# One issue order for all loads and copies of a recurrence-and-experts kernel, with the token numbers placed ahead of the gates

## The chip, the core and the metric

The kernel runs on one core of one Trainium2 chip. The metric is device microseconds of one execution, the median of three runs. TensorE is called PE here, VectorE DVE, ScalarE ACT, GpSimd POOL; SyncE (SP) computes nothing and issues DMA transfers.

## What is computed

The reference, cut to what matters:

```python
x, f_logit: (4, 5056, 256)          # batch, seq, d_model; all float32
sig = 1 / (1 + exp(-f_logit));  f = lower_bound + (1 - lower_bound) * sig;  i = 1 - f
for t in range(S):                  # a recurrence along the sequence
    h = f[:, t] * h + i[:, t] * x[:, t];  y[:, t] = h
x = y.reshape(20224, 256)           # tokens of the second half
logits = x @ w_gate                 # w_gate: (256, 8)
expert_idx = argmax(logits);  gate_w = softmax(logits)[expert_idx]
out = zeros((20224, 256))
for e in range(8):                  # w1: (8, 256, 1024), w2: (8, 1024, 256)
    tok_idx = tokens of e, the 80 with the largest gate_w
    out[tok_idx] = gate_w[tok_idx, None] * (relu(x[tok_idx] @ w1[e]) @ w2[e])
```

## The kernel before

The work has three stages. **Recurrence**: 40 units of 512 tokens (ten groups of the sequence times four batches). For each, SP loads 512 KB of `f_logit` (L227) and 512 KB of `x` (L229) into a ring of eight 512 KB slots, ACT, POOL, PE and DVE make the states `h_all` (which stay in SBUF, channels on partitions), and PE makes the logits. **Selection**: values per token and expert are turned by PE (`turn`, L440), DVE takes the eight largest of each part (`tops_of`, L447), and from these candidates the rank among rivals (L648, on DVE for the first `BY_DVE` columns and on ACT for the others), the flag `taken` (L654), the place `put` (L668) and, by 60 small PE products (L672), the table `kept`: row 0 holds the column numbers of the 80 tokens of each expert, row 1 their gate values. `trow` (L676) is row 0 as integers; `uncertain` (L567) makes flags for a rare second path. **Experts**: for each of eight, DVE, ACT and POOL copy the 80 token columns from `h_all` one by one (`gather`, L699; each engine first loads its numbers of `trow` into registers), POOL scales them (L711), PE makes the hidden layer (`hidden`, L716: 32 products per half, with weights taken at a stride of `CH` = 4 elements), ACT and DVE apply the relu, PE makes the result (`result`, L738), DVE copies it out of PSUM, and where 128 rows are complete `finish` turns them and multiplies by the gates (L762) and `scatter` writes them to `out` with an indirect DMA of POOL (L765).

The order of code is the order of each engine's queue. In the expert loop it is, for e = 0 to 7: gather(e+2), hidden(e+1), relu(e+1), result(e), scaled(e+2), then finish and, from e = 5 on, scatter. At e = 1 DVE also runs `rows_of` (L531), 14 small instructions that make `goal` (the rows of `out`) and `gates` from `slots`.

**Transfers.** `out` must be zero elsewhere, so besides the inputs 40 copies of zeros go from `out` to `out` (`copied`, L137; one of them, L157, from SBUF). The 32 halves of the weights (`half`, L495; 512 KB each) go to ring slots 1 to 7 in turn, in the order W1(0), W2(0), W1(1), then W1(e+1), W2(e): half number k takes the slot of half k - 7, so it waits until PE has used that. Seven halves (0 to 6) with three copies, then 12 copies (`SELECTING`) stand in SP's queue after the last unit; then each further half with one copy behind it (`more`, L769) until the copies are used up. Three transfers go through ACT's queue instead: `lb` and `wg` at the start (L94, L98), `flat_dram` (L524: `kept`, brought to SBUF as `flat` by ACT at L783, is written to DRAM), and the two reads of `slots` from it (L528).

The transfers of both queues take eight completion semaphores in rotation, and a transfer waits until the earlier one with its semaphore has landed. What is handed out in rotation isn't told by the code alone:

```python
for k, key in enumerate(halves_of[:NSLOT - 1]):      # L508
    if k % 2:
        copied()
    w_sb[key] = half(*key)
for _ in range(SELECTING):                           # 12
    copied()
```

Of the kernel before, what the change touches and what calls it, by code (L numbers as in the profile page):

```python
# [17 lines left out]
P = 128  # L18
# [8 lines left out]
def kernel(  # L27
# [24 lines left out]
    BY_DVE = 6  # L52
# [41 lines left out]
    nc.scalar.dma_start(out=lb, in_=lower_bound.rearrange("(o p) -> p o", p=P))  # L94
# [3 lines left out]
    nc.scalar.dma_start(out=wg[:, :, :E], in_=w_gate.rearrange("(o p) e -> p o e", p=P))  # L98
# [69 lines left out]
    with tc.tile_pool(name="gsm", bufs=1) as gsm:  # L168
# [9 lines left out]
        def masks():  # L178
            col_i = gsm.tile([P, P], I32, name="col_i", tag="ls")
            nc.gpsimd.iota(col_i, pattern=[[1, P]], base=0, channel_multiplier=0)  # L180
            make_identity(nc, ident)
            col_f = gsm.tile([P, P], F32, name="col_f", tag="col_f")
            low = row_i[:, 0:1]
            for k, (one, two, op, op2) in enumerate((
                    (shift_c, 0, ALU.arith_shift_right, ALU.bitwise_or),
                    (C - 1, 0, ALU.bitwise_and, ALU.bitwise_or),
                    (2, 1, ALU.arith_shift_right, ALU.bitwise_and),
                    (3, 1, ALU.arith_shift_right, ALU.bitwise_and))):
                nc.vector.tensor_scalar(row_i[:, ds(k + 1, 1)], low, one, two, op, op2)
# [13 lines left out]
            nc.vector.scalar_tensor_tensor(out=row_f[:, 2:3], in0=row_f[:, 4:5], scalar=-8.0,  # L203
                                           in1=row_f[:, 2:3], op0=ALU.mult, op1=ALU.add)
            nc.vector.tensor_scalar(nomlb, lb, 1.0, -1.0, ALU.mult, ALU.add)
            nc.vector.tensor_scalar(omlb, lb, -1.0, 1.0, ALU.mult, ALU.add)
# [12 lines left out]

# [123 lines left out]
        def sums(g0, g1):  # L343
            k = run(g0)
            ex = late_exp[:k, ds(LAST - g0, 1)]
            nc.vector.tensor_reduce(sums_t[:k, g0:g1], ex, AX.X, ALU.add)
# [46 lines left out]
        with tc.tile_pool(name="plg", bufs=1, space=PSUM) as plg, \  # L393
             tc.tile_pool(name="plt", bufs=1, space=PSUM) as plt:
            with tc.tile_pool(name="pss", bufs=2, space=PSUM) as pss, \
                 tc.tile_pool(name="psu", bufs=3, space=PSUM) as psu:
                for n in range(-AHEAD, n_unit):
                    unit(load, n + AHEAD)
                    m = n + AHEAD
                    if m == 3:  # L400
                        clear(early)
                    elif 3 < m < TURN and m % 4 == 3:
                        copied()
                    elif m == n_unit - 1:
                        for _ in range(3):
                            copied()
# [15 lines left out]
                    if n == n_unit - 2:  # L422
                        exponentials(LAST - 1, LAST)
                        for g0 in (0, 4):
                            summed(g0, g0 + 4)
                            valued(g0, g0 + 4, nc.gpsimd)
# [10 lines left out]
            with tc.tile_pool(name="pct", bufs=4, space=PSUM) as pct:  # L437
# [14 lines left out]
                a = turn((0, 4))  # L452
# [3 lines left out]
                tops_of(0)  # L456
                tops_of(2)
                some_of(-1)
                sums(LAST - 1, LAST)
                valued(LAST - 1, LAST, nc.vector)  # L460
                by_token(LAST)
                b = turn((4, 6))
                kept_values(a, 0, 4)
                shifted(LAST, n_grp)
                exponentials(LAST, n_grp)
                tops_of(4)
                c = turn((6, LAST - 1), (LAST - 1, LAST))
                kept_values(b, 4, 6)
                equals(LAST, n_grp)
                choice(LAST, n_grp, nc.vector)  # L470
                tops_of(6)
                sums(LAST, n_grp)
                valued(LAST, n_grp, nc.vector)
                d = turn((LAST, n_grp))
                tops_of(LAST - 1)
                tops_of(LAST)
# [17 lines left out]

    def half(which, e, i):  # L495
# [11 lines left out]
    SELECTING = 12  # L507
# [59 lines left out]
    def uncertain():  # L567
# [12 lines left out]
        nc.vector.tensor_scalar(d[:, 3:4], off[:, 2:3], float(capacity), off[:, 1:2],  # L580
                                ALU.min, ALU.not_equal)

    with tc.tile_pool(name="sel", bufs=1) as sel, \
# [17 lines left out]
        busy(psl, 1, "warm")  # L601
# [56 lines left out]
        nc.tensor.matmul(sums_p[:, 1:3], mates, count, start=True, stop=True)  # L658
        for engine, i, n in ((nc.vector, 0, 2), (nc.gpsimd, 2, 3)):
            engine.tensor_tensor(what[:, ds(i, n)], what[:, ds(i, n)],  # L660
                                 taken.unsqueeze(1).unsqueeze(3).broadcast_to([P, n, DEEP, E]),
                                 ALU.mult)
        off = consts.tile([P, 3], F32, name="off")
        nc.vector.tensor_copy(off, sums_p[:, :3])

        put = sel.tile([P, DEEP, K], BF16, name="put")
        at_slot = bass.AP(ahead.tensor, ahead.offset, [ahead.ap[0], (1, DEEP), (1, K)])
        nc.vector.tensor_scalar(put, at_slot, off[:, 0:1], None, ALU.is_equal)  # L668
        for i, terms_of in enumerate(((0, 1), (2, 3, 4))):
            for j in range(DEEP):  # L670
                for t in terms_of:
                    nc.tensor.matmul(kept[:, i], what[:, t, DEEP - 1 - j], put[:, j],  # L672
                                     start=j == 0 and t == terms_of[0],
                                     stop=j == DEEP - 1 and t == terms_of[-1])
        uncertain()
        nc.vector.tensor_copy(trow, kept[:, 0])  # L676
    selc.release()
# [7 lines left out]
    def experts(again):  # L685
        with tc.tile_pool(name="xp", bufs=3) as xp, \
# [29 lines left out]
            def hidden(e):  # L716
# [3 lines left out]
                ps = []  # L720
                for i in range(2):
                    h_ps = psh.tile([P, CH, K], F32, name="h_ps", tag="h_ps")
                    for c in range(CH):
                        for o in range(DC):
# [13 lines left out]
            def result(e):  # L738
                y_ps = psy.tile([P, DC, K], F32, name="y_ps", tag="y_ps")
                halves = [w.pop((2, e, i)) for i in range(2)]  # L740
                hid = HID.pop(e)
                for o in range(DC):
                    for c in range(FC):
                        for s in range(2):
                            nc.tensor.matmul(  # L745
                                y_ps[ds(s * H, H), o],
                                halves[c // CH][:, c % CH, ds(o * P + s * H, H)], hid[:, c],
                                start=c == 0, stop=c == FC - 1, skip_group_check=True)
                at = e * K % YR
                n = min(K, YR - at)  # L750
                nc.vector.tensor_copy(turned_y[:, :, ds(at, n)], y_ps[:, :, :n])  # L751
                if n < K:
                    nc.vector.tensor_copy(turned_y[:, :, ds(0, K - n)], y_ps[:, :, n:])
# [39 lines left out]
            if not again:  # L793
                read_slots()
# [3 lines left out]
            for e in range(E):  # L798
# [10 lines left out]
                if e == 1 and not again:  # L809
                    rows_of(consts)  # L810
# [3 lines left out]
                while e and (done + 1) * P <= (e + 1) * K:  # L814
# [99 lines left out]
```

## Time and profile before

| what | value |
|---|---|
| runs | 253.94, 254.63, 252.56 us; median 253.94 us |
| the profiled execution's own time | 252.7 us |
| its span, first to last instruction | 250.9 us |
| busy share of the span | PE 74%, DVE 64%, POOL 57%, ACT 53% |
| chain that ended last, by engine | PE 32%, DMA 32%, ACT 10%, DVE 9%, issue 8% |
| DMA | 80.66 MB, mean 322 GB/s |

The span is what the trace shows; 1.8 us of the profiled time lie around it. The recurrence lasts to about 127 us, the selection to 145 us, the experts and the scatters to the end. All times below are us from the span's start. SPq, ACTq, DVEq and POOLq are the instruction queues of these engines, in which DMA issues and register loads are seen.

### The profile page before, as it was taken

The numbers are of one execution on the slowest core, as the hardware profiler recorded it, in microseconds if no ns is written. First come the engines' busy times: TensorE is split into PE (matmuls) and PEld (weight loads), VectorE is DVE, ScalarE is ACT, GpSimd is POOL, SyncE is SP. The second block draws the span as 40 slices with busy tenths as digits, with TensorE's granted clock in tenths as the row PEclk, the third lists the DMA queues.
The fourth block names the chain that finished last, engine by engine and source line by source line (L and its number), as shares of the span: only waits on it lengthen the run. The fifth ranks groups of instructions, "written<-read, shape, count | busy, mean of one in ns | idle before, by whom it ended". The sixth has DMA issues, their size and how long they took to land.

```text
span 250.9 us, 7294 instructions
## 1 busy us (share of the span) xinstructions
PE 186.1 (74%) x2452; PEld 155.7 (62%) x2452; DVE 159.4 (64%) x404; ACT 132.9 (53%) x421; POOL 141.8 (57%) x286
## 2 busy tenths in 40 slices
PE   0798899899999998999956787570038859699920
PEld 1686777678768786877734446470037748689810
DVE  5288798999999999989988845414003741525210
ACT  4677787778887887888832445650005235050000
POOL 4778797889788878979662345652200045042121
PEclk9999999999999999999995997777558797899995
DMA  5999999999999999999870005889999999998310
GB/s 179 415 415 434 391 428 393 416 410 408 409 406 410 410 412 415 422 360 464 350 281 0 4 0 180 329 246 303 289 353 433 413 434 406 404 373 270 121 47 27
DMA packets 19686, 80.66 MB, mean 322 GB/s; under 512 B 4392, under 2 KB 4392, under 8 KB 19016
## 3 DMA queue, kind: packets, MB, share of 16 engines
q1 hardware_dynamic: 17520, 79.44, 81.4%
q0 software_dynamic: 240, 0.66, 0.7%
q8 instruction: 21, 0.34, 0.6%
q10 hardware_dynamic: 1880, 0.02, 0.4%
q14 instruction: 25, 0.20, 0.3%
HBM read 78.92 MB, written 21.37 MB: 400 GB/s over the span
## 4 chain that ended last, share of the span: by engine, by line
PE 32%; DMA 32%; ACT 10%; DVE 9%; issue 8%; POOL 3%; ACTq 2%; DVEq 1%; POOLq 0%; SPq 0%
DMA w_sb<-in_moe_w_dram 17%; PE sp L243 11%; PE up L251 9%; PE lg L281 6%; DMA f_t<-in_f_logit_dram 6%; ACT h_all L260 4%; ACT xe L707 3%; DMA out_dram<-out_dram 3%; DMA x_t<-in_x_dram 2%; DMA out_dram<-y,goal 2%; PE lt L305 2%; DVE h_all L268 2%; ACTq L703 2%; PE h_ps L727 2%; ACT ls L290 2%
## 5 line engine op out<-in xcount | busy, mean ns | idle before, releaser
L237 POOL TENSOR_TENSOR x_t<-f_t,x_t 128x1024 f32<-128x1024 f32 x40 | 94.9, 2373 | 21.6 <-DMA x_t<-in_x_dram 13.9
L268 DVE TENSOR_TENSOR_SCAN h_all<-h_all,up 128x512 f32<-128x512 f32 (+1 forms) x80 | 95.8, 1243 | 13.6 <-PE up L251 8.3
L727 PE MATMUL h_ps<-xe,w_sb 128*64 128x80 f32 x512 | 35.8, 319 | 29.5 <-DMA w_sb<-in_moe_w_dram 25.6
L260 ACT ACTIVATE h_all<-sp,nomlb 128x512 f32<-128x512 f32 (+1 forms) x80 | 50.1, 676 | 10.9 <-PE sp L243 10.9
L727 PEld LDWEIGHTS h_ps<-xe,w_sb 128*64 128x64 f32 x512 | 33.5, 222 | 31.9 <-DMA w_sb<-in_moe_w_dram 25.7
L233 ACT ACTIVATE f_t<-f_t 128x1024 f32<-128x1024 f32 x40 | 42.3, 1058 | 14.7 <-DMA f_t<-in_f_logit_dram 11.7
L243 PE MATMUL sp<-ident,f_t 128*128 128x128 f32 x320 | 45.2, 286 | 5.7 <-ACT f_t L233 5.7
L251 PE MATMUL up<-ident,x_t 128*128 128x128 f32 x320 | 44.3, 279 | 5.5 <-POOL x_t L237 3.2
L243 PEld LDWEIGHTS sp<-ident,f_t 128*128 128x128 f32 x320 | 35.8, 145 | 13.6 <-issue 12.5
L251 PEld LDWEIGHTS up<-ident,x_t 128*128 128x128 f32 x320 | 36.3, 142 | 9.0 <-POOL x_t L237 4.8
L707 ACT COPY xe<-h_all 128x2 f32 x256 | 25.4, 191 | 20.7 <-issue 20.2
L707 POOL COPY xe<-h_all 128x2 f32 x192 | 24.4, 193 | 14.7 <-issue 13.3
L707 DVE COPY xe<-h_all 128x2 f32 x192 | 22.7, 172 | 12.7 <-issue 12.7
L711 POOL TENSOR_TENSOR xe<-xe,omlb 128x160 f32<-128x160 f32 x8 | 3.6, 453 | 44.2 <-DVE xe L707 36.1
L281 PE MATMUL lg<-h_all,wg 128*32 128x128 f32 (+1 forms) x640 | 26.3, 282 | 0.0
L735 ACT ACTIVATE hid<-h_ps 128x320 f32<-128x320 f32 x8 | 3.5, 436 | 42.0 <-issue 36.4
L736 DVE TENSOR_SCALAR hid<-h_ps 128x320 f32<-128x320 f32 x8 | 3.9, 491 | 30.1 <-PE h_ps L727 30.1
L745 PE MATMUL y_ps<-hid,w_sb 128*64 128x80 f32 x512 | 21.7, 246 | 0.9 <-DMA w_sb<-in_moe_w_dram 0.8
L745 PEld LDWEIGHTS y_ps<-hid,w_sb 128*64 128x64 f32 x512 | 20.8, 149 | 1.6 <-DMA w_sb<-in_moe_w_dram 1.4
L281 PEld LDWEIGHTS lg<-h_all,wg 128*32 128x32 f32 x640 | 15.5, 108 | 6.1 <-issue 4.9
L751 DVE COPY turned_y<-y_ps 128x160 f32<-128x160 f32 (+1 forms) x8 | 2.6, 320 | 16.9 <-PE y_ps L745 16.9
L765 POOL DMA_INDIRECT out_dram<-y,goal x5 | 5.1, 1021 | 12.4 <-DMA out_dram<-y,goal 6.4
(127 smaller groups left out, 114.8 us busy)
## 6 DMA issues: line engine op xcount, KB each, us to landing
f_t<-in_f_logit_dram SPq DMA_DIRECT2D x40, 512.0 KB, 6.9
x_t<-in_x_dram SPq DMA_DIRECT2D x40, 512.0 KB, 7.2
out_dram<-out_dram SPq DMA_DIRECT2D x38, 512.0 KB, 9.0
w_sb<-in_moe_w_dram SPq DMA_DIRECT2D x32, 512.0 KB, 9.7
out_dram<-h_all SPq DMA_DIRECT2D x1, 512.0 KB
out_dram<-out_dram SPq DMA_DIRECT2D x1, 256.0 KB, 9.1
out_dram<-y,goal POOLq DMA_INDIRECT x5, 2.6
slots<-flat_dram ACTq DMA_DIRECT2D x2, 2.5 KB, 2.6
```

The lines of the kernel that those rows point to most:

```text
L233: nc.scalar.activation(s_t, s_t, ACT.Sigmoid, scale=-1.0)
L237: nc.gpsimd.tensor_tensor(u_t, sts[n], u_t, ALU.mult)
L243: nc.tensor.transpose(ps[:, ds(r * P, P)], sts[n][:, r, ds(o * P, P)], ident)
L251: nc.tensor.transpose(ps[:, r::R], uts[n][:, r, ds(o * P, P)], ident)
L260: nc.scalar.activation(columns(n, o).rearrange("p (k r) -> p k r", r=R), sps.pop((n, o)).rearrange("p (r k) -> p k r", r=R)[:, P - run(n / ...
L268: nc.vector.tensor_tensor_scan(h, h, ups.pop((n, o)), h_all[:, o, ds(spot(n - B) + G - 1, 1)] if n >= B else 0.0, ALU.mult, ALU.add)
L281: nc.tensor.matmul(lgs[g][ds(q * LC, LC), b, :k].rearrange("p (m i) -> p m i", i=2), wg[:, o], pairs[:, :, q], start=o == 0, stop=o == DC ...
L290: nc.scalar.copy(lss[g].rearrange("p (b t) -> p b t", b=B)[:, b0:b1], lgs[g][:, b0:b1, :k])
L707: copy(X[e][:, :, ds(k + j, 1)], h_all[:, :, ds(v, 1)])
L727: nc.tensor.matmul(h_ps[ds(s * H, H), c], wo[o][:, at:at + CH * (H - 1) + 1:CH], xt[:, o], start=o == 0, stop=o == DC - 1, skip_group_chec ...
L745: nc.tensor.matmul(y_ps[ds(s * H, H), o], halves[c // CH][:, c % CH, ds(o * P + s * H, H)], hid[:, c], start=c == 0, stop=c == FC - 1, ski ...
L765: nc.gpsimd.indirect_dma_start(out=out, out_offset=bass.IndirectOffsetOnAxis(ap=goal[:, ds(t, 1)], axis=0), in_=rows[0][:, t % R], in_offs ...
```

## The change

It has these parts.

1. `lb`, `wg`, `flat_dram` and `slots` are issued by SP: the first two after the loads of unit 1 (`small_loads`), `flat_dram` after 14 copies (`SELECTING` is 14 now) and ahead of half 7, and the reads of `slots` at e = 1, between halves 16 and 17.
2. `rows_of` moves from e = 1 to e = 3, and with it the first `finish`: two of them run at e = 3.
3. In the selection `placed(0, ...)` (24 products for the column numbers) goes ahead of `trow`, and `placed(1, ...)` (36 for the gates) behind it; POOL's share of the product with `taken` goes to DVE. One more rank column is ACT's (`BY_DVE` 5), a PE filler product goes ahead of the last `turn`, the sums and values of groups 4 to 7 and the order of the last group's steps change, and all `tops_of` follow each other. `flat` is one ACT copy.
4. For experts 4 to 7 a half of W2 is loaded as two blocks with runs of 2 KB per partition in place of 4 KB, and `hidden` takes W1 at a stride of 2 elements.
5. The last half is loaded as two transfers, the last `result` goes chunk by chunk over both output parts, and ACT copies one of the two.

```diff
-    BY_DVE = 6
+    BY_DVE = 5
-    nc.scalar.dma_start(out=lb, in_=lower_bound.rearrange("(o p) -> p o", p=P))
-    nc.scalar.dma_start(out=wg[:, :, :E], in_=w_gate.rearrange("(o p) e -> p o e", p=P))
+        def small_loads():
+            nc.sync.dma_start(out=lb, in_=lower_bound.rearrange("(o p) -> p o", p=P))
+            nc.sync.dma_start(out=wg[:, :, :E], in_=w_gate.rearrange("(o p) e -> p o e", p=P))
+            nc.vector.tensor_scalar(nomlb, lb, 1.0, -1.0, ALU.mult, ALU.add)
+            nc.vector.tensor_scalar(omlb, lb, -1.0, 1.0, ALU.mult, ALU.add)
...
                     m = n + AHEAD
+                    if m == 1:
+                        small_loads()
...
+    def rows_of_w2(e):
+
+        return CH if e < E // 2 else CH // 2
+
     def half(which, e, i):
...
-            nc.sync.dma_start(out=t, in_=w2[e][ds(i * FH, FH)].rearrange(
-                "(p j) d -> p (j d)", j=CH))
-            t = t.rearrange("p (j d) -> p j d", j=CH)
+            j = rows_of_w2(e)
+            to = t.rearrange("p (a x) -> p a x", x=j * D)
+            of = w2[e][ds(i * FH, FH)].rearrange("(a p j) d -> p a (j d)", p=P, j=j)
+            parts_of = CH // j if (e, i) == (E - 1, 1) else 1
+            for a in range(0, CH // j, CH // j // parts_of):
+                part = ds(a, CH // j // parts_of)
+                nc.sync.dma_start(out=to[:, part], in_=of[:, part])
+            t = t.rearrange("p (c d) -> p c d", d=D)
...
-    SELECTING = 12
+    SELECTING = 14
...
-        nc.scalar.dma_start(out=flat_dram.rearrange("(i e) k -> e i k", e=E), in_=flat)
+        nc.sync.dma_start(out=flat_dram.rearrange("(i e) k -> e i k", e=E), in_=flat)
...
-            nc.scalar.dma_start(out=slots[:, i], in_=flat_dram[ds(i * E, E)].rearrange(
+            nc.sync.dma_start(out=slots[:, i], in_=flat_dram[ds(i * E, E)].rearrange(
...
+        def with_taken(i, n):
+            nc.vector.tensor_tensor(what[:, ds(i, n)], what[:, ds(i, n)],
+                                    taken.unsqueeze(1).unsqueeze(3).broadcast_to([P, n, DEEP, E]),
+                                    ALU.mult)
...
+        placed(0, 0, 1)
+        with_taken(2, 3)
         uncertain()
         nc.vector.tensor_copy(trow, kept[:, 0])
+        placed(1, 2, 3, 4)
...
+                J = rows_of_w2(e)
...
-                                at = i * FH + c + CH * s * H
+                                at = i * FH + a * J * P + j + J * s * H
                                 nc.tensor.matmul(
-                                    h_ps[ds(s * H, H), c], wo[o][:, at:at + CH * (H - 1) + 1:CH],
+                                    h_ps[ds(s * H, H), c], wo[o][:, at:at + J * (H - 1) + 1:J],
...
-                for i in (0, 1):
-                    nc.scalar.copy(flat[:, i], kept[:, i])
+                nc.scalar.copy(flat, kept)
...
                 if e == 1 and not again:
-                    rows_of(consts)
+                    read_slots()
...
-                while e and (done + 1) * P <= (e + 1) * K:
+                if e == 3 and not again:
+                    rows_of(consts)
+                while e >= 3 and (done + 1) * P <= (e + 1) * K:
                     finish(done)
                     done += 1
```

SP's queue after the last unit, in the kernel before, from half 3 (L501) to half 6; L143 are the copies, L499 and L501 the halves of W1 and W2, and in brackets stand the semaphores that an issue waits for:

```order
L501 DMA w_sb<-in_moe_w_dram 128x1024 [waits DMAHW4_49,PE_49,Pool_49]
L499 DMA w_sb<-in_moe_w_dram 128x1024 [waits DMAHW6_49,PE_49]
L143 DMA out_dram<-out_dram 16x8192 [waits DMAHW0_49]
L499 DMA w_sb<-in_moe_w_dram 128x1024 [waits DMAHW1_49,PE_49,Pool_49]
L499 DMA w_sb<-in_moe_w_dram 128x1024 [waits DMAHW2_49,PE_49]
L143 DMA out_dram<-out_dram 16x8192 [waits DMAHW3_49]
```

In this rotation the issue of half 4 holds semaphore DMAHW6, which ACT's queue has for `flat_dram`, and numbers 5 and 7 are left out between rows, since they are ACT's too. The same place after the change, from half 4 (now L505) on, with the copies now L141:

```order
L505 DMA w_sb<-in_moe_w_dram 128x1024 [waits DMAHW4_49,PE_49]
L141 DMA out_dram<-out_dram 16x8192 [waits DMAHW5_49]
L505 DMA w_sb<-in_moe_w_dram 128x1024 [waits DMAHW6_49,PE_49,Pool_49]
L505 DMA w_sb<-in_moe_w_dram 128x1024 [waits DMAHW7_49,PE_49]
L141 DMA out_dram<-out_dram 16x8192 [waits DMAHW0_49]
```

The semaphores follow each other without a gap, each held by the SP transfer eight places ahead. Behind 14 copies follow, at the end of the selection:

```order
L141 DMA out_dram<-out_dram 16x8192 [waits DMAHW5_49]
L535 DMA flat_dram<-flat 8x2x80 [waits DMAHW6_49,Activation_49]
L505 DMA w_sb<-in_moe_w_dram 128x1024 [waits DMAHW7_49,PE_49]
L141 DMA out_dram<-out_dram 16x8192 [waits DMAHW0_49]
L513 DMA w_sb<-in_moe_w_dram 128x1024 [waits DMAHW1_49,PE_49]
```

The write of `flat_dram`, which waits for ACT's copy `flat`, has moved into SP's queue ahead of half 7 (L505), and all later transfers stand behind it.

DVE at the end of e = 3 (relu, result copied out, gates, then the register loads and the copies of gather(6)) in the kernel before:

```order
L736 TENSOR_SCALAR hid<-h_ps 128x320
L751 COPY turned_y<-y_ps 128x2x80
L762 TENSOR_SCALAR y<-t_ps,gates 128x256
L703 TENSOR_LOAD trow
L707 ISA
```

and after the change, from the last of the steps of `rows_of` on (ten more of them stand between the copy of the result and these):

```order
L568 TENSOR_REDUCE two_f<-past 128x5
L569 TENSOR_TENSOR goal<-far,two_f 128x5
L570 TENSOR_SCALAR gates<-slots 128x5
L571 RECIPROCAL gates<-gates 128x5
L793 TENSOR_SCALAR y<-t_ps,gates 128x256 x2
L721 TENSOR_LOAD trow
```

The 14 instructions of `rows_of` and a second product with the gates have come between the result of expert 3 and DVE's share of gather(6).

## Rows read from the trace of the kernel before

**Rows 1.** The page: GB/s that DMA moved in 40 equal slices of the span.
```profile
GB/s 179 415 415 434 391 428 393 416 410 408 409 406 410 410 412 415 422 360 464 350 281 0 4 0 180 329 246 303 289 353 433 413 434 406 404 373 270 121 47 27
```

**Rows 2.** Waits of SP's queue from 150 us: us in total, times, longest.
```profile
SPq L499 <- DMA flat_dram<-flat: 29.3, 1, 29.3
...
SPq L143 <- DMA slots<-flat_dram: 8.8, 2, 8.7
```

**Rows 3.** Timeline of SP's queue, 118 to 212 us: start, us, queue, line, operation, count.
```profile
122.88 0.33 SPq L501 DMA_DIRECT2D w_sb<-in_moe_w_dram  x1
152.59 0.33 SPq L499 DMA_DIRECT2D w_sb<-in_moe_w_dram  x1
...
172.19 0.33 SPq L499 DMA_DIRECT2D w_sb<-in_moe_w_dram  x1
...
183.82 0.52 SPq L143 DMA_DIRECT2D out_dram<-out_dram  x1
185.69 0.34 SPq L499 DMA_DIRECT2D w_sb<-in_moe_w_dram  x1
...
206.01 0.34 SPq L499 DMA_DIRECT2D w_sb<-in_moe_w_dram  x1
```

**Rows 4.** Stretches: us; PE, PEld, DVE, ACT, POOL busy; PE clock, DMA share, GB/s.
```profile
131.00:134.00 3.00, 0.45 (x1) 0.18 (x1) 2.45 (x10) 1.18 (x4) 0.00 (x0) 0.67 0.01 3
...
172.00:185.00 13.00, 0.00 (x0) 0.00 (x0) 0.59 (x6) 0.00 (x0) 3.46 (x25) 0.54 0.99 309
185.00:208.00 23.00, 17.03 (x290) 15.95 (x292) 9.75 (x69) 7.22 (x66) 3.46 (x25) 0.80 1.00 415
```

**Rows 5.** Waits of PE from 150 us: us in total, times, longest.
```profile
PE h_ps L727 <- DMA w_sb<-in_moe_w_dram: 25.6, 6, 17.9
```

**Rows 6.** Timeline, 136 to 165 us: end of the selection, first expert.
```profile
142.86 2.31 PE L672 MATMUL kept<-put,what 128*8 128x80 bf16 x60 [0.94 <-DVE put L668]
...
145.21 0.23 DVE L676 CAST trow<-kept 8x80 int32<-8x80 f32 x1 [1.40 <-PE kept L672]
...
150.93 0.33 ACT L783 COPY flat<-kept 8x80 f32<-8x80 f32 x2
...
151.66 4.43 PE L727 MATMUL h_ps<-xe,w_sb 128*64 128x80 f32 x64 [2.00 <-POOL xe L711]
...
160.29 4.28 PE L727 MATMUL h_ps<-xe,w_sb 128*64 128x80 f32 x60 [1.68 <-DMA w_sb<-in_moe_w_dram]
```

**Rows 7.** Timeline, 165 to 200 us: result(0), and first and last of 14 `rows_of` instructions.
```profile
164.76 2.85 PE L745 MATMUL y_ps<-hid,w_sb 128*64 128x80 f32 x58
...
192.92 0.16 DVE L540 CAST rcol_i<-slots 128x5 int32<-128x5 f32 x1
...
195.09 0.19 DVE L560 RECIPROCAL gates<-gates 128x5 f32<-128x5 f32 x1
```

**Rows 8.** Timeline, 200 to 251 us: last experts and the five scatters.
```profile
222.91 0.29 DVE L751 COPY turned_y<-y_ps 128x128 f32<-128x128 f32 x1 [1.90 <-PE y_ps L745]
...
223.62 4.07 PE L727 MATMUL h_ps<-xe,w_sb 128*64 128x80 f32 x64
223.74 0.48 DVE L762 TENSOR_SCALAR y<-t_ps,gates 128x256 f32<-128x256 f32 x1 [0.43 <-PE t_ps L760]
225.52 2.80 DVE L707 COPY xe<-h_all 128x2 f32 x24 [1.30 <-issue]
...
227.52 2.38 PE L745 MATMUL y_ps<-hid,w_sb 128*64 128x80 f32 x64
...
229.72 1.21 POOL L765 DMA_INDIRECT out_dram<-y,goal  x1 [0.77 <-issue]
...
235.59 0.97 POOL L765 DMA_INDIRECT out_dram<-y,goal  x1 [4.66 <-DMA out_dram<-y,goal]
...
238.27 0.97 POOL L765 DMA_INDIRECT out_dram<-y,goal  x1 [1.71 <-DMA out_dram<-y,goal]
...
245.49 0.97 POOL L765 DMA_INDIRECT out_dram<-y,goal  x1 [3.08 <-DVEq L827]
```

More of the change, by code (lines that the diff above doesn't have):

```diff
@@ L344, in sums @@
             k = run(g0)
-            ex = late_exp[:k, ds(LAST - g0, 1)]
+            ex = late_exp[:k, ds(LAST - g0, 1)] if g0 >= LAST - 1 else shifts[:k, g0:g1]
             nc.vector.tensor_reduce(sums_t[:k, g0:g1], ex, AX.X, ALU.add)
@@ L423 @@
                         exponentials(LAST - 1, LAST)
-                        for g0 in (0, 4):
-                            summed(g0, g0 + 4)
-                            valued(g0, g0 + 4, nc.gpsimd)
+                        summed(0, 4)
+                        valued(0, 4, nc.gpsimd)
                     unit(logits, n - 1)
@@ L450, in tops_of @@
                     peaks(cts[g0][0], cts[g0][1], i)
-                a = turn((0, 4))
                 aside(LAST, 0, B - 1)
@@ L455 @@
                 aside(LAST, B - 1, B)
-                tops_of(0)
-                tops_of(2)
                 some_of(-1)
+                sums(4, LAST - 1)
                 sums(LAST - 1, LAST)
-                valued(LAST - 1, LAST, nc.vector)
+                valued(4, LAST - 1, nc.gpsimd)
+                valued(LAST - 1, LAST, nc.gpsimd)
                 by_token(LAST)
+                a = turn((0, 4))
+                shifted(LAST, n_grp)
+                exponentials(LAST, n_grp)
                 b = turn((4, 6))
                 kept_values(a, 0, 4)
[L464 to L468, printed above, removed]
                 equals(LAST, n_grp)
                 choice(LAST, n_grp, nc.vector)
-                tops_of(6)
                 sums(LAST, n_grp)
                 valued(LAST, n_grp, nc.vector)
+                c = turn((6, LAST - 1), (LAST - 1, LAST))
+                busy(plt, 1, "lt")
+                kept_values(b, 4, 6)
                 d = turn((LAST, n_grp))
-                tops_of(LAST - 1)
-                tops_of(LAST)
+                for lo, _ in parts:
+                    tops_of(lo)
                 kept_values(c, 6, LAST)
@@ L579, in uncertain @@
                                        op0=ALU.is_le, op1=ALU.mult)
-        nc.vector.tensor_scalar(d[:, 3:4], off[:, 2:3], float(capacity), off[:, 1:2],
+        totals = sel.tile([P, 2], F32, name="totals")
+        nc.vector.tensor_copy(totals, sums_p[:, 1:3])
+        nc.vector.tensor_scalar(d[:, 3:4], totals[:, 1:2], float(capacity), totals[:, 0:1],
                                 ALU.min, ALU.not_equal)
@@ L600 @@
             ("rivals", M), ("rivals2", M), ("sums_p", 4)))
-        busy(psl, 1, "warm")
         for r in (rivals2, rivals):
@@ L657, with placed @@
         nc.tensor.matmul(sums_p[:, 0:1], before, count[:, 0:1], start=True, stop=True)
[L658 to L669, printed above, removed]
+        def with_taken(i, n):
+            nc.vector.tensor_tensor(what[:, ds(i, n)], what[:, ds(i, n)],
+                                    taken.unsqueeze(1).unsqueeze(3).broadcast_to([P, n, DEEP, E]),
+                                    ALU.mult)
+        def placed(i, *terms_of):
             for j in range(DEEP):
@@ L674 @@
                                      stop=j == DEEP - 1 and t == terms_of[-1])
+        with_taken(0, 2)
+        off = consts.tile([P, 1], F32, name="off")
+        nc.vector.tensor_copy(off, sums_p[:, :1])
+        nc.tensor.matmul(sums_p[:, 1:3], mates, count, start=True, stop=True)
+        put = sel.tile([P, DEEP, K], BF16, name="put")
+        at_slot = bass.AP(ahead.tensor, ahead.offset, [ahead.ap[0], (1, DEEP), (1, K)])
+        nc.vector.tensor_scalar(put, at_slot, off, None, ALU.is_equal)
+        placed(0, 0, 1)
+        with_taken(2, 3)
         uncertain()
         nc.vector.tensor_copy(trow, kept[:, 0])
+        placed(1, 2, 3, 4)
     selc.release()
@@ L738, in result, with product @@
             def result(e):
-                y_ps = psy.tile([P, DC, K], F32, name="y_ps", tag="y_ps")
                 halves = [w.pop((2, e, i)) for i in range(2)]
                 hid = HID.pop(e)
[L742 to L748, printed above, removed]
+                last = e == E - 1
+                y = psy.tile([P, DC, K], F32, name="y_ps", tag="y_ps")
+                ys = [y[:, o] for o in range(DC)]
+                if last:
+                    ys[1] = psh.tile([P, CH, K], F32, name="h_ps", tag="h_ps")[:, 0]
+                def product(o, c):
+                    for s in range(2):
+                        nc.tensor.matmul(
+                            ys[o][ds(s * H, H)], halves[c // CH][:, c % CH, ds(o * P + s * H, H)],
+                            hid[:, c], start=c == 0, stop=c == FC - 1, skip_group_check=True)
+                for k in range(DC * FC):
+                    product(*(divmod(k, FC) if not last else reversed(divmod(k, DC))))
                 at = e * K % YR
                 n = min(K, YR - at)
-                nc.vector.tensor_copy(turned_y[:, :, ds(at, n)], y_ps[:, :, :n])
+                if last:
+                    assert n == K
+                    nc.vector.tensor_copy(turned_y[:, 0, ds(at, n)], ys[0])
+                    nc.scalar.copy(turned_y[:, 1, ds(at, n)], ys[1])
+                    return
+                nc.vector.tensor_copy(turned_y[:, :, ds(at, n)], y[:, :, :n])
                 if n < K:
-                    nc.vector.tensor_copy(turned_y[:, :, ds(0, K - n)], y_ps[:, :, n:])
+                    nc.vector.tensor_copy(turned_y[:, :, ds(0, K - n)], y[:, :, n:])
             def finish(t):
@@ L793, in experts @@
             if not again:
-                read_slots()
                 total = psm.tile([1, 4], F32, name="total", tag="total")
```

3 lines of the change are left out of this document (1 added, 2 removed).

## The prediction, made before the change was timed

> **What bounds the kernel now.** I read the page's slices first. DMA moves some 410 GB/s through the recurrence, then nothing for three slices of 6.3 us, then 180 to 350 for six, and full rate again only from slice 31 [rows 1]. The queue's own waits say why: SP waited 29.3 us at one issue of a weight half, and the releaser is the landing of `flat_dram` [rows 2]. In the timeline half 3 goes out at 122.88 and half 4 at 152.59 [rows 3], while DMA is idle by 131 [rows 4]. Half 4 and the copies behind it have nothing to do with `flat_dram`; they share a completion semaphore with it, as the order of the queues shows. The reads of `slots` do the same to two later copies for 8.8 us [rows 2]. So about 22 us of transfers that could have run beside the selection run behind it. The bill comes in the experts: PE waits 25.6 us for weights, 17.9 in one piece [rows 5]. PE's busy share hides this. The path after the selection is thus the DMA stream, and at the end a chain on DVE and POOL.
>
> **Part 1, one order: the stream worked out.** I sum it in span time. Two pitches are needed. A semaphore comes free when the transfer eight places ahead has landed, so spacings of issues are spacings of landings. From 172.19 to 183.82 copies land alone: eight issues, seven gaps, 1.66 us each. From 185.69 to 206.01 halves and copies alternate: 17 issues, 16 gaps, 1.27 each [rows 3]. The rates of the two stretches, 309 and 415 GB/s, agree [rows 4].
>
> At 131 the old stream had ended with half 3. Now half 4, a copy, halves 5 and 6 follow (4 x 1.27 = 5.1) and 14 copies alone (23.2): 159.3. `flat_dram` needs ACT's `flat`, ready at 151.3 before [rows 6], and is tiny, so it is covered by the copies in front of it. Half 7 needs the slot that hidden(0) frees, at 156.1 before [rows 6], also covered. Half 7, copy, half 8, copy: 164.4. Half 9 needs result(0), which ended at 167.6 [rows 7]; of that 1.7 was hidden(1) waiting for weights [rows 6], and the selection gives about 1.7 (below): 164.2, just in time. From there 17 transfers bring half 17, the second of W2(3): 164.4 + 17 x 1.27 = 186.0, and 1.3 for the reads of `slots` between and the landing (bounds 0 and 3): 187.3. Half 31 is 14.5 later in the count: 205.7. All slots on the way are free in time, since each half needs only what PE used seven halves earlier.
>
> A rule speaks against this gain. The Trainium skill ("DMA: Bandwidth & Descriptors", section "Issuing engines are not separate DMA queues") says that transfers run on the same 16 DMA engines whichever engine issues them, and that spreading issues only saves issue time. By that the move is worth next to nothing; it is rival C below. This trace shows the other part: it is not the engines that were shared badly but the waits.
>
> **Part 3, the selection.** 60 products take 2.31 us ahead of `trow` [rows 6]; 24 take 0.9, so 1.4 goes. One rank column fewer on DVE and a filler product fewer ahead of the rivals give some tenths, the product with `taken` for three terms costs DVE some tenths ahead of `trow`. I take 1.7 (bounds 0 and 3). The stream covers most of it: with 0, result(0) frees half 9 at 165.9 and the end is 1.5 later. `lb` landing behind four loads, the order of the last sums, one `flat` copy: half a microsecond either way, covered by the same stream, which is full through the recurrence.
>
> **Part 2, the late `rows_of`.** This costs, and on the path. result(3) waits for half 17, of which only its last three quarters are left then (1.8 of the 2.38 us that 64 result products take [rows 8]): 189.1. DVE copies it out (189.5), runs the 14 instructions, 192.92 to 195.28 in the trace [rows 7], 2.4: 191.9. The first product with the gates (0.48 [rows 8]) ends at 192.4; the second turn needs the one PSUM buffer, so PE turns until 192.9, and hidden(5), whose weights landed some 3 us earlier, stands behind it on PE. Behind the second product (193.4) DVE makes gather(6): 1.30 + 2.80 [rows 8], 197.5. Before, this sat at e = 1 and in gaps.
>
> **Part 4, runs of 2 KB.** Two effects. PE: 64 hidden products take 4.07 us at a stride of 4, 64 result products 2.38 with contiguous weights [rows 8]. The trace has no stride of 2, so hidden(4) to hidden(7) lie between 2.4 and 4.1; I take the middle, 3.2. The Trainium skill ("SBUF — State Buffer", section "Door 1: The DMA port swizzle") gives lines of 16 bytes and full rate from two hits per line. A stride of 2 floats has two, a stride of 4 one; by it hidden falls to 2.4, and the forecast would be 0.8 lower. The trace agrees in so far as stride 4 is the slower. DMA: a transfer with runs of 32 KB was not faster than one with 4 KB [rows 3], so I take 0 for 2 KB. Were each of the eight halves to cost double, half 31 would land at 216, and part 5 plus the scatters would still cover most of it: at most 1.6 later.
>
> **The tail.** hidden(5) 192.9 to 196.1, result(4) to 198.5. From the copy of result(4) to the first scatter the trace has 222.91 to 229.72, 6.8: DVE's copy and gates, its gather(7), POOL's scaling [rows 8]. So scatter 0 goes at 205.4. From there to the end it was 250.9 - 229.72 = 21.2, one scatter behind the landing of the other: 226.6. But scatter 0 to 1 took 5.9 and 1 to 2 took 2.7 [rows 8], and four weight halves were under way at the first. Now the last one lands as scatter 0 starts, so up to 3.2 may go; I take half: 225.0. The profiled time is 1.8 more than its span: **226.8 us**, against 252.7 profiled; the median of the runs is 253.94, within their spread.
>
> Part 5 is worth nothing here: hidden(7) starts after scaling at 204.6, result(7) ends at about 212.6 and its rows are ready by 214.2, while scatter 4 can't go before 205.4 + 15.8 - 1.6 = 219.6. If the scatter chain were shorter by 5 us, it would count.
>
> **Rivals.**
>
> A (forecast, 0.68): 226.8, own range 222 to 231.
>
> B (0.14), the stream is slower. If copies keep 1.66 also between weights, 17 transfers cost 6.6 more: 233.4. For: copies alone, DMA fully busy, ran so [rows 4]. Against: the alternating stretch is the very pattern that comes.
>
> F (0.12), the tail is shorter. If gates and gather(6) find gaps (3.3), hidden takes 2.4 (0.8) and no weight disturbs the scatters (1.6): 221.1. For: in-order queues leave gaps where PE waits. Against: the one PSUM buffer.
>
> C (0.03), the change doesn't do what it says: the issue waits elsewhere, and only the 1.7 of the selection is left: 251.0. For: 23 halves still wait for slots. Against: in the new order no semaphore is shared with a later transfer of another queue.
>
> D (0.03), slower: all 25 later halves now stand behind one issue that waits for ACT's `flat`. From 159.3 on each microsecond that it is late costs one. To lose more than the 26 gained, `flat` would have to come after 185; it came at 151.3 [rows 6], so ACT's gather would have to be held by the busy DMA for 34 us. Transfers ran beside all engines throughout the recurrence [rows 1] without such a hold. If it happened, say at 189, the time is 256.5.
>
> **How the numbers follow.** A, B and F hold 0.94. The range takes in F's 221.1 and B's 233.4: 220.5 to 234. C is within 1% (the runs spread by 0.8%, so about 1% is what a measurement of this kernel can tell from no change), D slower: faster 0.94, same 0.03, slower 0.03.
>
> **What would show it.** DMA at 300 to 415 GB/s without an empty slice from 125 to 200; no wait of SP on `flat_dram` over 10 us, and the write behind 14 copies at about 150; half 7 issued near 155 and not at 172; PE's longest wait for weights under 6 us; `rows_of` near 190 and hidden(5) behind two turns; hidden(4) to (7) at 2.4 to 4.1; scatter 0 near 205 and the next 3 to 6 later. Wrong it would be if slices near 140 to 150 were still empty, if PE waited over 10 us for half 17, or if scatter 4 followed result(7) at once.

## The result and the profile after

The kernel after takes **228.59 us** (median of four runs, 228.2 to 230.06); the kernel before, run beside it, 253.45. The ratio is 0.903, 95% interval 0.897 to 0.909: some 25 us faster. 226.8 was forecast, range 220.5 to 234. The profiled execution took 230.06 us with a span of 228.3. One execution of experiment 8 (234.15 us) and one of experiment 12 (232.79 us) ran slow, and the medians there leave it out.

The page's slices, GB/s of DMA, to hold against [rows 1]:

```profile
GB/s 232 335 422 414 414 409 420 408 412 411 392 416 404 411 376 414 417 409 384 411 455 358 425 434 375 353 333 296 332 400 451 401 334 394 127 366 279 41 44 26
```

The three empty slices are gone. One low slice is new, 127 GB/s, the 35th, from 194 to 200 us. The waits of SP's queue, and of PE, from 120 us on (us in total, times, longest), answer to [rows 2] and [rows 5]:

```profile
SPq L513 <- PE h_ps L747: 10.0, 2, 7.2
...
SPq L505 <- PE h_ps L747: 4.0, 2, 3.6
...
SPq L535 <- ACT flat L813: 0.7, 1, 0.7
```

```profile
PE h_ps L747 <- DMA w_sb<-in_moe_w_dram: 5.4, 4, 2.0
PE y_ps L769 <- DMA w_sb<-in_moe_w_dram: 3.5, 3, 2.0
PE t_ps L791 <- DVE y L793: 2.9, 1, 2.9
```

The 29.3 us for `flat_dram` are gone: its write itself waits 0.7 us for ACT. PE's 17.9 us for weights have become waits of at most 2.0. SP's longest wait ahead of a transfer, 7.2 us, is now for a ring slot that hidden(5) holds, and this is the low slice. The timeline of SP's queue (start, us) answers to [rows 3]:

```profile
123.35 0.33 SPq L505 DMA_DIRECT2D w_sb<-in_moe_w_dram  x1
...
128.75 18.59 SPq L141 DMA_DIRECT2D out_dram<-out_dram  x14
149.07 0.34 SPq L535 DMA_DIRECT2D flat_dram<-flat  x1
153.37 0.36 SPq L505 DMA_DIRECT2D w_sb<-in_moe_w_dram  x1
```

Half 4 goes out at 123.35, not 152.59, and half 7 at 153.37, not 172.19. The timeline of PE around `rows_of`, then of POOL's scatters, answers to [rows 7, 8]:

```profile
186.87 3.46 PE L769 MATMUL y_ps<-hid,w_sb 128*64 128x80 f32 x48 [1.96 <-DMA w_sb<-in_moe_w_dram]
...
193.62 0.62 PE L791 MATMUL t_ps<-ident,turned_y 128*128 128x128 f32 x2 [2.91 <-DVE y L793]
194.17 3.85 PE L747 MATMUL h_ps<-xe,w_sb 128*64 128x80 f32 x64
...
201.00 2.44 PE L747 MATMUL h_ps<-xe,w_sb 128*64 128x80 f32 x64
```

```profile
207.09 1.22 POOL L796 DMA_INDIRECT out_dram<-y,goal  x1 [0.78 <-SPq L858]
211.48 0.98 POOL L796 DMA_INDIRECT out_dram<-y,goal  x1 [3.17 <-DMA out_dram<-y,goal]
215.20 0.97 POOL L796 DMA_INDIRECT out_dram<-y,goal  x1 [2.75 <-DMA out_dram<-y,goal]
219.59 0.97 POOL L796 DMA_INDIRECT out_dram<-y,goal  x1 [3.42 <-DMA out_dram<-y,goal]
223.17 0.97 POOL L796 DMA_INDIRECT out_dram<-y,goal  x1 [2.60 <-DMA out_dram<-y,goal]
```

PE waits 2.9 us for the late gates ahead of hidden(5), which takes 3.85 us; hidden(6), with the same stride, takes 2.44. All four later scatters wait for the landing of the one before: this chain ends the kernel.

### The profile page after: what moved, and what is told of

Read it like the earlier page. It is cut to its first block, busy times and chain, and to the rows that moved or that the text cites. A ratio compares the mean times of both kernels' runs of the same rounds, so it can differ in the third digit from the quotient of the medians.

```text
span 228.3 us, 7296 instructions
## 1 busy us (share of the span) xinstructions
PE 179.4 (79%) x2452; PEld 149.5 (66%) x2452; DVE 160.3 (70%) x404; ACT 133.5 (58%) x423; POOL 140.3 (61%) x283
## 5 line engine op out<-in xcount | busy, mean ns | idle before, releaser
L245 PE MATMUL sp<-ident,f_t 128*128 128x128 f32 x320 | 46.0, 289 | 7.0 <-ACT f_t L235 5.6
L253 PE MATMUL up<-ident,x_t 128*128 128x128 f32 x320 | 45.1, 283 | 4.0 <-DVE h_all L270 2.9
L245 PEld LDWEIGHTS sp<-ident,f_t 128*128 128x128 f32 x320 | 36.4, 147 | 15.1 <-issue 12.7
L253 PEld LDWEIGHTS up<-ident,x_t 128*128 128x128 f32 x320 | 37.2, 145 | 6.9 <-DVE h_all L270 4.4
L747 PE MATMUL h_ps<-xe,w_sb 128*64 128x80 f32 x512 | 28.1, 273 | 7.4 <-DMA w_sb<-in_moe_w_dram 5.4
L747 PEld LDWEIGHTS h_ps<-xe,w_sb 128*64 128x64 f32 x512 | 26.6, 186 | 9.6 <-DMA w_sb<-in_moe_w_dram 4.3
L725 DVE COPY xe<-h_all 128x2 f32 x192 | 22.6, 173 | 12.9 <-issue 10.7
L769 PEld LDWEIGHTS y_ps<-hid,w_sb 128*64 128x64 f32 x480 | 19.9, 149 | 4.2 <-DMA w_sb<-in_moe_w_dram 3.4
L307 PE MATMUL lt<-ident,ls 128*128 128x128 f32 (+1 forms) x40 | 7.5, 310 | 4.3 <-ACT ls L292 4.3
```

Source lines behind the costliest of these rows:

```text
L245: nc.tensor.transpose(ps[:, ds(r * P, P)], sts[n][:, r, ds(o * P, P)], ident)
L253: nc.tensor.transpose(ps[:, r::R], uts[n][:, r, ds(o * P, P)], ident)
L307: nc.tensor.transpose(lts[g0][:k, g - g0, j], ls[:, j::R], ident)
L725: copy(X[e][:, :, ds(k + j, 1)], h_all[:, :, ds(v, 1)])
L747: nc.tensor.matmul(h_ps[ds(s * H, H), c], wo[o][:, at:at + J * (H - 1) + 1:J], xt[:, o], start=o == 0, stop=o == DC - 1, skip_group_check= ...
L769: nc.tensor.matmul(ys[o][ds(s * H, H)], halves[c // CH][:, c % CH, ds(o * P + s * H, H)], hid[:, c], start=c == 0, stop=c == FC - 1, skip_ ...
```

## The experiments

Times are medians; "the kernel after" is 228.59 us.

**1. Before, with `flat_dram` and `slots` on POOL's queue.** Is it the shared completion semaphore, or the one order?

```diff
-        nc.scalar.dma_start(out=flat_dram.rearrange("(i e) k -> e i k", e=E), in_=flat)
+        nc.gpsimd.dma_start(out=flat_dram.rearrange("(i e) k -> e i k", e=E), in_=flat)
...
-            nc.scalar.dma_start(out=slots[:, i], in_=flat_dram[ds(i * E, E)].rearrange(
+            nc.gpsimd.dma_start(out=slots[:, i], in_=flat_dram[ds(i * E, E)].rearrange(
```

> The kernel before, with the write of flat_dram and the reads of slots issued by POOL instead of ACT; POOL has no other transfer that is issued before the scatters. Theory (the half's 29.3 us wait came from completion counts that ACT's transfers share with SP's halves, not from the order of issue): with POOL's transfers counted apart the half no longer waits for flat_dram, half 4 is issued near 124 us where it was 152.6, no slice of the page between 130 and 152 us falls below 250 GB/s, and the time is 228 to 235 us. Rival (what counts is that everything goes through one queue in one order): the gap stays and the time is 248 us or more.

231.2 us, ratio 0.910 (0.907 to 0.913). SP's queue:

```profile
122.33 0.33 SPq L499 DMA_DIRECT2D w_sb<-in_moe_w_dram  x1
...
127.08 15.66 SPq L143 DMA_DIRECT2D out_dram<-out_dram  x12
155.52 0.33 SPq L499 DMA_DIRECT2D w_sb<-in_moe_w_dram  x1
```

Half 4 goes out at 122.33. SP has no wait for `flat_dram` any more. Another issuing engine for three small transfers gives 22.6 of some 25 us, with nothing put in one order, so the shared semaphores were the cause. One detail was missed: the slice from 149 to 155 us falls to 118 GB/s, since 12 copies run out before hidden(0) frees a slot; the change has 14.

**2. After, with the two back on ACT's queue.**

```diff
-        nc.sync.dma_start(out=flat_dram.rearrange("(i e) k -> e i k", e=E), in_=flat)
+        nc.scalar.dma_start(out=flat_dram.rearrange("(i e) k -> e i k", e=E), in_=flat)
...
-            nc.sync.dma_start(out=slots[:, i], in_=flat_dram[ds(i * E, E)].rearrange(
+            nc.scalar.dma_start(out=slots[:, i], in_=flat_dram[ds(i * E, E)].rearrange(
```

> The kernel after, with the write of flat_dram and the reads of slots issued by ACT again; all other parts of the change stay. Theory (this one part makes the gain): SP waits 20 us or more for flat_dram again, the DMA engines have slices near empty before 150 us, and the time is 243 to 252 us. Rival (the numbers ahead of the gates, the shorter runs and the chunks of the last result make a good part of the gain): 235 us or less.

252.12 us, ratio 0.994 (0.991 to 0.997), at the upper edge of what was expected. SP's waits:

```profile
SPq L141 <- DMA flat_dram<-flat: 25.9, 1, 25.9
```

The wait is back, at a copy instead of a half, and all other parts together are worth under 2 us while it stands.

**3. After, with the old end of the selection** (60 products ahead of `trow`, POOL's share, `BY_DVE` 6).

```diff
-    BY_DVE = 5
+    BY_DVE = 6
...
-        with_taken(0, 2)
...
-        placed(0, 0, 1)
-        with_taken(2, 3)
...
-        placed(1, 2, 3, 4)
...
+        for engine, i, n in ((nc.vector, 0, 2), (nc.gpsimd, 2, 3)):
...
+        for i, terms_of in enumerate(((0, 1), (2, 3, 4))):
```

> The kernel after, with the end of the selection as before: all 60 products of the kept rows ahead of the gates' sums, the factor applied in two pieces on DVE and POOL, 6 of the 24 numbers' comparisons as before. Theory (the weights' stream covers the selection): hidden(0) starts about 2 us later, hidden(5) at most 0.7 us later, and the time is 0 to 1 us above the kernel after. Rival (the selection is on the path that sets the end): the whole 2.2 us are lost, 230.5 to 231 us.

230.53 us, ratio 0.909 (0.903 to 0.915). hidden(0) starts 1.4 us later (150.90), hidden(5) 0.8 (195.01). By medians this is 1.9 us, by ratios 0.9 to 1.5, and the intervals overlap: between the two expectations, so the stream covers it in part at most.

**4. After, with 4 KB runs for all experts.**

```diff
-        return CH if e < E // 2 else CH // 2
+        return CH
```

> The kernel after, with runs of 4 KB for all eight experts (the weights of a product lie 4 elements apart, not 2; the last expert's second half is one transfer). Theory (the distance of the weights' elements sets the rate at which PE loads them, while runs of 2 KB cost the transfers nothing): hidden(6) and hidden(7) take 4.0 to 4.2 us where they took 2.44, hidden(5) stays at 3.9 to 4.4, and the time is 2 to 3.5 us above the kernel after, as far as the chain of the scatters doesn't hide it. Rival 1 (the chain of the scatters hides all of it): within 0.7 us. Rival 2 (runs of 2 KB slow the stream by more than they give back): 1 us or more faster.

228.55 us, ratio 0.900 (0.897 to 0.902): no difference. The theory fell to its first rival. PE's timeline from hidden(5), and two of the scatters:

```profile
193.70 4.36 PE L747 MATMUL h_ps<-xe,w_sb 128*64 128x80 f32 x64
...
201.48 4.07 PE L747 MATMUL h_ps<-xe,w_sb 128*64 128x80 f32 x64
```

```profile
207.57 1.21 POOL L796 DMA_INDIRECT out_dram<-y,goal  x1 [0.78 <-issue]
...
222.86 0.97 POOL L796 DMA_INDIRECT out_dram<-y,goal  x1 [2.75 <-DMA out_dram<-y,goal]
```

hidden(6) is 1.6 us longer, yet the last scatter goes as early as in the kernel after: only hidden(5) lies ahead of the first scatter, what follows stands beside the chain. What hidden(5) costs stays open: the execution compared here ran it at TensorE's low clock (3.85 us); against the repeat (experiment 9), where it took 2.44, the last scatter is 1.9 us later, while the medians are equal.

**5 to 8. The tail.** These edits are to the expert loop. In experiment 5 `slots` is read, `rows_of` run and the first rows finished one expert earlier:

```diff
+                if e == 0 and not again:
                     read_slots()
...
-                if e == 3 and not again:
+                if e == 2 and not again:
                     rows_of(consts)
-                while e >= 3 and (done + 1) * P <= (e + 1) * K:
+                while e >= 2 and (done + 1) * P <= (e + 1) * K:
```

> The kernel after, with the read of slots, the products of rows_of and the first turn of finished rows one expert earlier (ahead of hidden(4) instead of hidden(5)). Theory (the late rows_of holds hidden(5) by 3 us, and PE's idle time there is followed by its lower clock): hidden(5) starts by 191.5 us where it was 194.2 and takes 2.4 to 2.6 us where it took 3.85, the slice near 127 GB/s is gone, and the time is 3 to 4.5 us below the kernel after. Rival (the read of slots lands late, so hidden(4) is held instead of hidden(5)): the time is within 1 us.

225.37 us, ratio 0.891 (0.886 to 0.895): 3.2 us less, as expected. The slice with 127 GB/s is gone, and hidden(5) follows the turn at once:

```profile
190.26 0.45 PE L791 MATMUL t_ps<-ident,turned_y 128*128 128x128 f32 x2 [0.43 <-DVE turned_y L782]
190.63 2.44 PE L747 MATMUL h_ps<-xe,w_sb 128*64 128x80 f32 x64
```

In experiment 6 the first scatter goes one expert earlier:

```diff
-                while e + 3 >= E and put_out < done:
+                while put_out < (done if e + 3 >= E else 1 if e + 4 == E else 0):
```

> The kernel after, with the first scatter issued one expert earlier, behind result(4), before result(5). Theory (the five scatters run one after another, each held by the one before, so the end is the first scatter plus 21.2 us): the first scatter starts near 201 to 203 us where it was 207.1, and the time is 3 to 4.5 us below the kernel after. Rival 1 (the end is set by the last result's rows, not by the chain): the last scatter starts at the same time, within 0.7 us. Rival 2 (the scatter disturbs the last weights): 0.5 to 2 us slower.

226.07 us, ratio 0.893 (0.889 to 0.897): 2.5 us less, under the 3 to 4.5 expected, though the first scatter goes 7.4 us earlier (5.7 against the repeat):

```profile
199.67 1.21 POOL L796 DMA_INDIRECT out_dram<-y,goal  x1 [0.78 <-issue]
...
206.55 1.01 POOL L796 DMA_INDIRECT out_dram<-y,goal  x1 [0.74 <-DMA out_dram<-y,goal]
210.83 0.98 POOL L796 DMA_INDIRECT out_dram<-y,goal  x1 [3.28 <-DMA out_dram<-y,goal]
```

The chain sets the end, but its length isn't fixed: 6.9 us from the first scatter to the second, where it was 4.4. The last weights are under way then.

Experiment 7 has both edits.

> Both of the two edits above in one kernel: rows_of one expert earlier and the first scatter one expert earlier. Theory (each takes a hold of its own away from one chain): the gains add up to 6 to 8 us, 220.5 to 222.5 us, unless the last weights set the end: they landed at 210.4, and hidden(7), result(7), the last turn and one scatter with its landing behind them take 2.4 + 2.4 + 1.5 + 5, which bounds the end at about 222. Rival (the two remove the same hold): no better than the better one of the two.

223.71 us, ratio 0.882 (0.877 to 0.887): better than either, 4.9 us in all where 6 to 8 were expected. Again the first two gaps of the chain are long (scatters at 197.81, 203.29, 208.02).

Experiment 8 leaves these out and puts products without use into the loop over `result`'s products `k`:

```diff
                 for k in range(DC * FC):
+                    if e == 3 and k == CH and not again:
+                        busy(psm, 5, "total")
```

> The kernel after, with 5 products without use on PE in the middle of result(3), while it waits for its last weights, so that PE has less idle time there. Theory (PE's idle time ahead of the second half of result(3) is followed by the lower clock, at which its products take 72 ns instead of 37): the granted clock between 186.5 and 190.5 us is 0.9 or more where it was 0.64, rows_of, hidden(5) and the first scatter come 1 to 2 us earlier, and the time is 1 to 2 us below the kernel after. Rival (the lower clock has another cause, or 5 products are too few): the clock there stays near 0.64 and the time within 0.5 us.

229.70 us, ratio 0.907 (0.902 to 0.911): no gain. The clock in result(3) did rise, 48 products took 1.88 us and not 3.46, but the five products took 4.56 us and result(3) ended 1.4 us later than without them. hidden(5) behind its idle wait took 3.62 all the same.

**9 to 12. The chain spread out.** Experiment 9 is the kernel after again, on the chip of the next three; it is called the repeat.

> The kernel after, unchanged, to have it beside the next three on the same chip. Theory and rival alike: 228 to 230 us, ratio to the kernel before 0.90 to 0.906.

228.59 us again, ratio 0.905 (0.900 to 0.910).

In experiment 10 every scatter goes as soon as its rows are finished, on top of experiment 7:

```diff
-                while put_out < (done if e + 3 >= E else 1 if e + 4 == E else 0):
+                while put_out < min(done, e - 2):
```

> The kernel with rows_of and the first scatter one expert earlier, and besides every scatter as soon as its rows are finished: the first behind result(3), then one behind each result. Theory (the end is a chain of five scatters, 4 to 5.5 us each, until the last result's rows become later than the chain): the first scatter starts near 192.5 to 194 us, the first four are done before the last rows are ready, the last one starts near 212.5 to 213.5 us, and the end is 5.5 us behind it: span 218 to 219.5, time 219.5 to 221.5 us. Rival (a scatter on POOL's queue holds the gathers behind it, so hidden(6) and hidden(7) come later): 222.5 us or more.

**219.81 us**, ratio 0.868 (0.864 to 0.873): the fastest kernel here, some 33 us below the one before. What POOL waits for from 185 us on, in the kernel after and here:

```profile
POOL out_dram L796 <- DMA out_dram<-y,goal: 11.9, 4, 3.4
```

```profile
POOL out_dram L796 <- DVE y L793: 9.3, 2, 6.9
...
POOL out_dram L796 <- DMA out_dram<-y,goal: 1.0, 1, 1.0
```

The two waits put down to rows are those of the last two scatters, 3 and 4 (counted from 0). For scatter 3 this is right: its rows are ready at 210.54, it goes at 210.82, and scatter 2 had landed at 209.23. For scatter 4 it is doubtful. The end of the chain that ended last (start, us, what):

```profile
202.88 6.35 DMA out_dram<-y,goal
...
210.82 2.58 DMA out_dram<-y,goal
...
213.96 0.30 POOLq L857
214.25 0.90 POOL out_dram L796
```

Scatter 3 lands at 213.40 and scatter 4 goes 0.77 us later; in the kernel after, too, 0.77 us lie between the landing of scatter 3 (222.40) and the start of scatter 4 (223.17), and there its rows had long been ready. So the chain is broken once, ahead of scatter 3, and its last link still stands. The first scatter goes at 188.47, 4 us earlier than expected, and the first three land after 6.2 to 6.5 us, where 4 to 5.5 were expected. The gathers weren't held: hidden(6) and hidden(7) start as in experiment 5. The last scatter goes at 214.17, 0.7 later than expected, behind a stop of PE of 1.85 us in result(6) for which the profile shows no releaser (see the last section).

Experiment 11 adds the edit of experiment 4 to it.

> The kernel with rows_of and all scatters early, and runs of 4 KB for all eight experts. Theory (the distance of the weights' elements sets the length of hidden, and its gain was hidden only by the chain of scatters): hidden(5) to hidden(7) take 4.0 us each where they take 2.44, all of it ahead of the last scatter, so 4 to 5 us slower than with runs of 2 KB, 224 to 226 us. Rival (the stream of weights or the gathers give back what PE loses): within 1.5 us of it.

222.54 us, ratio 0.879 (0.875 to 0.884): with the chain broken ahead of scatter 3 the stride is worth 2.7 us, in place of 4 to 5. hidden(5) to (7) take 4.29, 4.07 and 4.00, 5.0 us more than in experiment 10; its profile doesn't have the stop just named, which accounts for part of the rest between the two profiles.

Experiment 12 takes the chunks of the last result out of experiment 10:

```diff
-                last = e == E - 1
+                last = False
...
-            parts_of = CH // j if (e, i) == (E - 1, 1) else 1
+            parts_of = 1
```

> The kernel with rows_of and all scatters early, and the last result as before: its second half in one transfer, column half by column half, one move of both halves to turned_y. Theory (with the chain of scatters out of the way, the last result's weights landing late and its last move lie on the path): 0.5 to 1.5 us slower than with chunks. Rival (the last weights land before hidden(7) ends, so chunks have nothing to gain): within 0.5 us.

220.90 us, ratio 0.870 (0.865 to 0.875), against 0.868 with chunks. The medians are 1.1 us apart, the ratios 0.5, and the intervals overlap; the last scatters of the two profiles start within 0.1 us, here too 0.77 us behind the landing of the scatter before (213.30), so in these two executions the last rows did not set the end. Whether chunks gain anything is left open.

## Why the prediction was right

- **What bounds the kernel, and part 1.** Right, in size too. Half 17 landed by 186.87 (187.3 forecast), `flat_dram` was written at 149.07 ("about 150"), half 7 went at 153.37 ("near 155"). That half 17 came within 0.5 us is in part luck, since the terms were off both ways: by the landings in the trace half 3 came at 132.45 (131 taken) and halves and copies in turn took 1.35 us each (1.27 taken), while the 14 copies alone took 1.50 (1.66 taken). Experiments 1 and 2 show that the shared semaphores were the cause, and that this one part carries nearly all of the gain: 22.6 of some 25 us.
- **The rivals.** Rival C: refuted here as a forecast. The Trainium skill ("DMA: Bandwidth & Descriptors", section "Issuing engines are not separate DMA queues") says that spreading issues over engines only saves issue time. But 22 us hung on whose completion an issue had to wait for, of which the rule says nothing. Rivals B and D did not come: the stream took 1.35 us a transfer, not 1.66, and the write waited 0.7 us for `flat`. Of F only the hidden of 2.4 us came.
- **Part 3.** `trow` came 2.2 us earlier (143.04), where 1.7 was taken. Without it the end was to be 1.5 later; experiment 3 measured 0.9 to 1.9.
- **Part 2.** Right: hidden(5) at 194.17 (192.9 forecast) behind `rows_of` and two turns. Experiment 5 prices the lateness at 3.2 us. What was not foreseen is TensorE's clock. In the profiled execution PE waited 1.96 us for weights, then ran the 48 products of result(3) at 72 ns each (3.46 / 48), and later hidden(5) at 3.85; the repeat shows how it is without. Windows of the kernel after, then of the repeat (us; PE, PEld, DVE, ACT, POOL busy; clock, DMA share, GB/s):

```profile
186.00:190.00 4.00, 3.13 (x48) 3.13 (x48) 0.00 (x0) 2.00 (x22) 2.03 (x16) 0.61 1.01 379
...
194.00:198.00 4.00, 4.00 (x72) 3.83 (x72) 2.43 (x18) 0.44 (x1) 0.00 (x0) 0.61 0.36 142
```

```profile
182.00:186.00 4.00, 3.73 (x69) 3.73 (x71) 1.58 (x14) 0.44 (x1) 0.98 (x6) 0.62 0.95 299
186.00:190.00 4.00, 2.51 (x64) 2.20 (x59) 0.63 (x2) 3.13 (x32) 2.56 (x21) 1.00 0.86 326
...
194.00:198.00 4.00, 4.00 (x120) 3.97 (x116) 2.70 (x24) 1.40 (x12) 0.00 (x0) 1.00 0.87 305
```

  1.00 is the upper level, 2.4 GHz; a window with 0.61 was mostly at the lower one, 1.2 GHz. In the repeat the clock fell earlier, in a stretch that the weights cover, and the first scatter went at 205.35, the forecast's 205.4, with a span of 226.0 where 225.0 was forecast. That the start agrees is luck: hidden(5) began 0.6 us later than forecast (193.48) and was 0.8 shorter (2.44).
- **Part 4.** The size of hidden was wrong: the middle of 3.2 was taken, 2.44 was measured at full clock, the low end that the rule of the Trainium skill ("SBUF — State Buffer", section "Door 1: The DMA port swizzle": two hits per 16-byte line are enough) gave. What it was worth to the end was nothing measurable here (experiment 4), 2.7 us once the chain was broken (experiment 11).
- **The tail.** The failed step is "up to 3.2 may go; I take half". Scatter 0 to 1 did shrink, from 5.87 to 4.39, but from there to scatter 4 it took 11.7 in place of 9.9 [rows 8], and the chain was 21.2 again in the profiled execution, 20.65 in the repeat. The landings of scatters 1 and 2 grew from 2.4 us each before to 3.5 and 3.6, although the weights had landed by then; why is open. In the profiled execution the later first scatter (207.09, by the clock) and this chain (21.2 where 19.6 was taken) are the 3.3 us by which the span is above its forecast; in the repeat the chain alone is the 1.0. The median lies between, 1.8 above.
- **Part 5.** Nothing was forecast and the profile agrees: scatter 4 waits for scatter 3, long after its rows are ready. That chunks would count with a chain shorter by 5 us was not confirmed (experiment 12): the last scatter still waited for the one before.

## What to carry to other kernels

When an engine's queue waits for a transfer that it doesn't need, look at which completion semaphore the wait is on: one small late transfer on another queue can hold a whole stream through a shared one, and moving that transfer, to the same queue or to one that counts apart, took off 22 us or more here. Once a stream is full, look for what is issued late in the tail: here small DVE work sat one expert and the scatters up to two later than their data allowed, and moving them took off 8.8 us more. A chain of dependent transfers can hide gains on another engine (2.7 us on PE here), so test such gains again when the chain is shorter.

## What was not expected of the hardware

- The same kernel, profiled twice, had TensorE's low clock at different places from 182 to 198 us (186 to 190 and 194 to 198; 182 to 186). The first scatters are 1.7 us apart, the spans 2.3. PE had waited 2 us for weights ahead of 186.87 in the one and 182.27 in the other, but a like wait of 2.0 us ahead of 181.47 in the first was followed by the full clock (60 products of hidden(4) in 2.30 us); the wait of 2.9 us ahead of hidden(5) was followed by the low clock in one and not in the other. What decides is open.
- The landing of a scatter of 128 rows took 2.4 to 4.1 us in the kernel after, and 5.0 to 7.0 for the first three of experiments 10 to 12, which ran beside the weights.
- PE stopped for 1.85 us in result(6) in experiment 10, and for 2.0 and 1.2 in experiment 12, with nothing in the profile that released it. The trace points to PE's own code. The stops lie behind the same instruction of PE's stream, the 4801st, in both experiments, and behind the 4545th, 256 earlier, in experiment 12 (weight loads counted too); and each ends 1.4 to 1.5 us after a transfer of queue q8 (kind "instruction", 16 KB each, 21 in an execution), which began at 206.01, and at 200.00 and 205.80. In experiments 5, 7, 9 and 11 and in the kernel after, which don't stop there, PE reaches the same two places 1.65 to 3.7 us after such a transfer ended. So PE most likely waited for its next instructions; no run here tests it.
